# Layer A of an interleaved attention kernel: the third round's output scaled into the key tile, a value tail copy moved into the next segment, and the first Wo round moved behind the fourth Q

## The chip, the cores and the metric

The kernel runs on one core of a Trainium2 chip. Its metric is the device time of one execution in microseconds (us), and the median over several executions counts. One execution was also taken by the hardware profiler. Its page and its trace are what is read below. Engine names are those of the profile: PE (TensorE matmuls), PEld (its weight loads), DVE (VectorE), ACT (ScalarE), POOL (GpSimd), SP (SyncE, which here only issues DMAs).

## The reference

Four residual layers A, B, A, B work on x of 2048 rows by 640 columns. The change touches only layer A, a recurrent attention with 32 heads of 192 columns. Cut to what matters:

```python
for s in range(n_seg):                       # 64 segments of 32 rows, one after the other
    xs = x[:, s*32:(s+1)*32]                 # x is already layer-normed
    h = concatenate([mem, xs], axis=1)       # 8 memory rows + 32 rows
    q, k, v = h @ Wq, h @ Wk, h @ Wv         # per head
    p = softmax(where(mask, q @ k.T * scale, -1e9))
    o = (p @ v) @ Wo
    mem = o[:, :8]                           # the next segment needs this
    outs.append(o[:, 8:])
```

The memory rows make the 64 segments of a layer a serial chain: the first Q product of a segment cannot start before the Wo product of the segment ahead is complete.

## The kernel before

**Stages.** For each A layer `A_pre` projects, for all segments at once, the last 8 rows of each segment, which don't depend on the memory, and stores them in DRAM as `kqb` (Q and K) and `vb` (V). `A_chain` then runs the 64 segments. In a segment it handles 8 memory rows and the first 24 of the 32 rows, and takes the last 8 rows ("tails") from DRAM. The Wo product of the tails is made later in layer B from `otb`. Layer B is not touched.

**Rounds.** A segment has four rounds of eight heads, in the order 0, 1, 2, 3 in even and 3, 2, 1, 0 in odd segments. `order[0]` to `order[3]` name them here, and `L` is 3. Each round has a Q, a K and a V projection (`project`, L953, 20 matmuls each, with the stationary tile `hT`), scores (`scores`, L988 and L993), an exponential (`weigh`, L999), row sums (`sums`, L1004), the product with V (`attend`, L1018), reciprocals of the sums (`reciprocals`, a logarithm at L1009 and an exponential at L1010 on ACT), a scaling of the product into SBUF (`scale_out`, L1026 and twice L1030 on DVE) and a Wo product (`wo_round`, L1046, 24 matmuls) that accumulates over the four rounds in the PSUM tile `W`.

**Order.** The schedule is manual: each engine runs its instructions in the order of the program text, and waits are made from the data and from the reuse of tiles.

**Tiles.** Most tiles have a single buffer. `OT` (128 x 6 x 80) receives the scaled output of every round, feeds `wo_round`, feeds the tail copy of `store_tail` (L1035 on POOL, then a DMA), and holds the raw first Q of the next segment. `KT` (128 x 6 x 96) holds the transposed keys of the round. Its columns 0 to 63 are written by DVE (L968), and 16 of its columns 64 to 95 by POOL from `kqb` (`extra_kq`, L925, called by `next_kq`). `rc` holds the reciprocals, also in one buffer. `Vs` (named `Vp` in the profile) holds the values: partitions 0 to 63 those of the segment's own rows, 64 to 95 the tails in use, 96 to 127 the next tails from DRAM. `place_v` copies 96 to 127 down to 64 to 95 on POOL (L936) and issues the next fetch (`fetch_v`, L932). It runs twice in a segment.

**Weights.** Most of Wq, Wk and Wv stays in SBUF. Three of the five row blocks of each, for the first and the last round, share slots: as soon as the first round's projection has read a slot, SP loads the last round's piece into it (`load_slot`, L623). In the next segment the last round comes first. Wo works alike: rounds 1 and 2 are resident, rounds 0 and 3 share `wo_end`. After the first Wo round SP loads six pieces of the last round's rows (`load_wo`, L640, 320 KB each), which the fourth Wo round reads at the segment's end.

**Segment end.** After the last Wo round DVE transposes `W` (L1183), adds its halves into the first 8 columns of `hT` (L1186, four instructions with both inputs in SBUF), and the next segment's first Q can start. The first pair of L1186 releases its first 12 matmuls, the second pair the rest. `keep_busy` (L1054) puts matmuls whose result isn't used between the third and the fourth Wo round (8) and behind the fourth (16). The rows of a finished segment are added up at the start of the next by `keep_rows` (L905, L908) and stored by `store_rows` (L912, a DMA that POOL issues).

Of the kernel before, what the change touches and what calls it, by code (L numbers as in the profile page):

```python
# [115 lines left out]
class Kernel:  # L116
# [746 lines left out]
    def A_chain(self, xn_dram, at_dram, li, load_slot, piece, load_wo, late_wo, wo_mid, wo_end, low):  # L863
        nc, tc, KC, NSEG = self.nc, self.tc, self.KC, self.NSEG
        scale = float(self.Dh) ** -0.5
        NR = 4
        with tc.tile_pool(name=f"A{li}_ch", reuse_waits="tile", bufs=1) as sp, \
# [3 lines left out]
            KT = sp.tile([P, 6, 96], BF16, name="KT")  # L871
            QT = sp.tile([P, 2, 4, 80], BF16, name="QT")
            Vs = sp.tile([P, 896], BF16, name="Vp")
            OT = sp.tile([P, 6, 80], BF16, name="OT")
            for i, t in enumerate((KT, QT, Vs)):
                (nc.vector if i % 2 else nc.gpsimd).memset(t[:], 0.0)
            at_rows = self.attn_rows
# [33 lines left out]
            def store_rows(s, io):  # L911
                nc.gpsimd.dma_start(out=at_rows[32 * s:32 * s + 32, :].rearrange("t (g c) -> g t c", g=4), in_=io[:, :])  # L912
# [22 lines left out]
            def place_v():  # L935
                nc.gpsimd.tensor_copy(out=Vs[64:96, :], in_=Vs[96:P, :])  # L936
                fetch_v()
# [64 lines left out]
            def sums(S, E):  # L1002
                one = self.ones_blk[0:96, :]
                nc.tensor.matmul(S[:, 0:320], lhsT=ap3(one, [list(one.ap[0]), [0, P]]), rhs=E[0:96, 0:320], start=True,  # L1004
                                 stop=True, skip_group_check=True)
# [14 lines left out]
                                         stop=(k == 192), skip_group_check=True)  # L1020
                return O

            def scale_out(O, rc):
                rv = rc[:, :].rearrange("p (x e q) -> p x e q", e=2, q=80)
                ov = O[:, 0:480].rearrange("p (c q) -> p c q", q=80)
                nc.vector.tensor_tensor(out=OT[:, 0:4, :], in0=ov[:, 0:4, :],  # L1026
                                        in1=rc[:, :].rearrange("p (c q) -> p c q", q=80), op=ALU.mult)
                for e in range(2):
                    h = slice(64 * e, 64 * e + 64)
                    nc.vector.tensor_tensor(out=OT[h, 4:6, :], in0=ov[h, 4:6, :], in1=rv[h, :, e, :], op=ALU.mult)  # L1030

            def store_tail(s, r, tag="otb"):
                q0 = 64 - 64 * (r % 2)
                ob = sp.tile([P, 96], BF16, name="otb", tag=tag)
                nc.gpsimd.tensor_copy(out=ob[:, :].rearrange("p (c q) -> p c q", q=16), in_=OT[:, :, q0:q0 + 16])  # L1035
                nc.gpsimd.dma_start(out=self.otb_d[s, :, 96 * r:96 * r + 96], in_=ob[:, :])  # L1036

            def wo_round(W, r, first, last):
                m0 = 16 * (r % 2)
                w = wo_end[:, :] if r in (0, 3) else wo_mid[:, 7680 * (r - 1):7680 * r]  # L1040
                for j in range(0, 12, 2):
                    for g in range(4):
                        i = j + g // 2
                        G, c = (i // 4, i % 4) if i < 8 else (i % 4 // 2, 4 + i % 2)
                        wi = w[:, 640 * i:640 * i + 640].rearrange("p (h e c) -> p e h c", h=2, e=2)
                        nc.tensor.matmul(W[32 * g:32 * g + 32, 0:320], lhsT=OT[:, c, m0 + 32 * G:m0 + 32 * G + 32],  # L1046
                                         rhs=wi[:, g % 2], start=(first and j == 0), stop=(last and j == 10),
                                         tile_position=(0, 32 * g), skip_group_check=True)
# [33 lines left out]
            hx_transpose(hT, xr)  # L1082
            W = None
            for s in range(NSEG):
                order = rounds(s)
                L = NR - 1

                def q_or_k(m, n):
                    ps = pqp.tile([P, 512], F32, name="ps_qk", tag="qk")
                    project(hT, ps, m, n, s)  # L1090
                    return to_raw(ps, "raw" if n else "OT" if m == "Q" else "rc")

                def values(n, pool, tag):
                    pv = pool.tile([P, 512], F32, name="ps_v", tag=tag)
                    project(hT, pv, "V", n, s)
                    return pv

                if s > 0:
                    io = keep_rows(W)
                raw = q_or_k("Q", 0)  # L1100
                to_rows(raw, "Q", order[0])
                if s == 0:
                    fill(FILL[li])
                to_rows(q_or_k("K", 0), "K")
                if s == 0:
                    late_wo(2)
                if s > 0:
                    store_rows(s - 1, io)
                W = pop.tile([P, 512], F32, name="ps_w", tag="w")
                raw = q_or_k("Q", 1)  # L1110
                pv = values(0, pop, "v")
                v_rows(pv, 0, "s")
                v_rows(pv, 1, "s")
                S = scores(order[0])
                to_rows(raw, "Q", order[1])
                next_kq(s, 0)
                E = weigh(S)
                to_rows(q_or_k("K", 1), "K")
                for n in range(1, L):
                    raw = q_or_k("Q", n + 1)  # L1120
                    sums(S, E)
                    O = attend(E)
                    if n == 2:
                        place_v()
                    S1 = scores(order[n])
                    rc = reciprocals(S)
                    E = weigh(S1)
                    S = S1
                    to_rows(raw, "Q", order[n + 1])
                    next_kq(s, n)  # L1130
                    if n == 1 and s + 1 < NSEG:
                        xr = load_rows(s + 1)
                    if n == L - 1:
                        to_rows(q_or_k("K", n + 1), "K")
                        scale_out(O, rc)
                    else:
                        rawk = q_or_k("K", n + 1)
                        scale_out(O, rc)
                        to_rows(rawk, "K")
                    store_tail(s, order[n - 1])  # L1140
                    pv = values(n, pop, "v")
                    v_rows(pv, 0, "s")
                    v_rows(pv, 1, "s")
                    if n < L - 1:
                        wo_round(W, order[n - 1], n == 1, False)
                        if n == 1:
                            load_wo(order[L])
                            if s == NSEG - 1:
                                load_wo(3, low[:, 0:7680])
                pv = values(L, pqp, "qk")  # L1150
                sums(S, E)
                O = attend(E)
                S1 = scores(order[L])
                rc = reciprocals(S)
                E = weigh(S1)
                v_rows(pv, 1, "v")
                v_rows(pv, 0, "s")
                wo_round(W, order[L - 2], False, False)
                sums(S1, E)
                O1 = attend(E)  # L1160
                if s + 1 < NSEG:
                    hT = new_hT()
                    hx_transpose(hT, xr)
                scale_out(O, rc)
                store_tail(s, order[L - 1], "raw")
                next_kq(s, L)
                if s + 1 < NSEG:
                    place_v()
                wo_round(W, order[L - 1], False, False)
                rc = reciprocals(S1)  # L1170
                scale_out(O1, rc)
                idle = pop.tile([P, 512], F32, name="ps_idle", tag="v")
                keep_busy(idle, 2)
                wo_round(W, order[L], False, True)
                if s + 1 < NSEG:
                    keep_busy(idle, 4)
                store_tail(s, order[L])
                fill(SEG_FILL)
                if s + 1 < NSEG:
                    wt = sp.tile([P, 2, KC, 32], F32, name="wt", tag="rc")  # L1180
                    wv = W[:, 0:320].rearrange("p (h j b) -> p h b j", h=2, b=KC)
                    for b0, b1 in ((2, 5), (0, 2)):
                        nc.vector.transpose(out=wt[:, :, b0:b1, :], in_=wv[:, :, b0:b1, :])  # L1183
                        for h in range(2):
                            a, b = slice(64 * h, 64 * h + 64), slice(64 - 64 * h, 128 - 64 * h)
                            nc.vector.tensor_tensor(out=hT[a, b0:b1, 0:8], in0=wt[a, h, b0:b1, 0:8], in1=wt[b, h, b0:b1, 0:8],  # L1186
                                                    op=ALU.add)
# [72 lines left out]
```

## Time and profile before

| what | value |
|---|---|
| median of 3 runs | 3846.09 us (3836.32 to 3852.01) |
| profiled execution | 3840.06 us, span 3838.3 us |
| granted PE clock over the span | 0.98 |
| first chain: L1183, first and last start | 213.2 to 1588.1 us, 63 segments |
| second chain ends with its last Wo matmul at | 3534.8 us |
| PE busy in the span | 3457.9 us (90%) |
| DMA read and written | 853.72 MB and 73.40 MB, 242 GB/s over the span |

The two chains take some 2790 of 3838 us, and a segment takes about 22.2 us: (1588.1 - 213.2) us over 62 steps. What a change inside the segment brings is multiplied by 126, the number of steps from one segment to the next in both layers. The timeline of one engine lists its instructions in order of time. Its columns are start, duration, engine, line, operation, output and inputs, the shape, the number of merged instructions, and in brackets the idle time ahead of them with what ended it.

### The profile page before, as it was taken

What the parts mean: (1) busy time and instruction counts of PE and PEld (TensorE: products, weight loads), DVE (VectorE), ACT (ScalarE), POOL (GpSimd) and SP (SyncE); (2) the same over time, 40 slices, a digit from 0 to 9 for tenths busy, and PEclk for the clock granted to TensorE, in tenths of its full rate; (3) what the DMA queues carried; (4) which work ended last, traced back from release to release, by engine and by line L of the source; (5) the groups of instructions that cost most, each with busy time, mean ns of one, the idle gap of its engine ahead of it and who ended that gap; (6) DMA issues with size and microseconds to landing.
All of it is one profiled execution on the core that took longest, in us unless ns stands there. A gap on an engine that the chain in (4) does not pass through costs nothing. (4 is left out here: it accounts for less than half of the span.)

```text
span 3838.3 us, 147201 instructions
## 1 busy us (share of the span) xinstructions
PE 3457.9 (90%) x60042; PEld 2134.0 (56%) x60222; DVE 2243.8 (58%) x5940; ACT 1986.4 (52%) x4517; POOL 1958.4 (51%) x4871
## 2 busy tenths in 40 slices
PE   9989989989889989889899899998989899998898
PEld 6755555555555555555377555555555555555553
DVE  5456666666666666546633566666566666665465
ACT  2345555555555555545423455555555555555453
POOL 3455656655655656530433565565555565664300
PEclk9999999999999999999899999999999999999999
DMA  8978878788878878830477787887887788888300
GB/s 302 314 269 282 275 264 286 272 272 275 275 264 285 273 262 289 291 100 1 144 257 219 273 283 264 284 283 260 271 280 265 260 289 274 274 278 289 100 1 28
DMA packets 531681, 933.29 MB, mean 243 GB/s; under 512 B 145459, under 2 KB 295691, under 8 KB 531003
## 3 DMA queue, kind: packets, MB, share of 16 engines
q1 hardware_dynamic: 428858, 818.87, 61.9%
q0 software_dynamic: 68480, 91.75, 8.2%
q10 hardware_dynamic: 33664, 13.24, 1.4%
q8 instruction: 472, 7.73, 0.8%
q14 instruction: 207, 1.69, 0.1%
HBM read 853.72 MB, written 73.40 MB: 242 GB/s over the span
## 5 line engine op out<-in xcount | busy, mean ns | idle before, releaser
L953 PEld LDWEIGHTS <-hT 128*32 128x32 bf16 x30720 | 785.9, 96 | 654.2 <-DVE hT L1186 198.6
L953 PE MATMUL ps_qk<-arena,hT 128*32 128x384 bf16 x20480 | 992.3, 328 | 112.0 <-DVE hT L1186 96.5
L963 ACT ACTIVATE raw<-ps_qk 128x384 bf16<-128x384 f32 x896 | 440.0, 491 | 435.7 <-PE ps_qk L953 207.0
L1046 PE MATMUL ps_w<-arena,OT 128*32 128x320 bf16 x12288 | 549.9, 305 | 107.8 <-DVE OT L1026 68.8
L953 PE MATMUL ps_v<-arena,hT 128*32 128x384 bf16 x10240 | 503.3, 327 | 43.2 <-DMA arena<-in_A_Wv_dram 41.6
L980 ACT ACTIVATE Vp<-ps_v 64x384 bf16<-64x384 f32 x896 | 434.0, 484 | 72.2 <-PE ps_v L953 40.9
L972 DVE STREAM_TRANSPOSE QT<-raw 128x256 bf16<-128x256 bf16 x384 | 171.0, 445 | 489.9 <-PE ps_s L993 459.5
L1046 PEld LDWEIGHTS <-OT 128*32 128x32 bf16 x12288 | 260.2, 96 | 346.6 <-DVE OT L1026 168.7
L968 DVE STREAM_TRANSPOSE KT<-raw 128x384 bf16<-128x384 bf16 x512 | 296.2, 579 | 174.2 <-ACT raw L963 166.2
L916 POOL DMA_DIRECT2D kqb<-kqb x512 | 286.6, 560 | 163.9 <-POOL KT L925 115.4
L1036 POOL DMA_DIRECT2D otb<-otb x512 | 283.3, 553 | 169.6 <-POOL otb L1035 148.1
L1026 DVE TENSOR_TENSOR OT<-ps_o,rc 128x320 bf16<-128x320 f32 x512 | 251.8, 492 | 149.3 <-ACT rc L1010 55.2
L1030 DVE TENSOR_TENSOR OT<-ps_o,rc 64x160 bf16<-64x160 f32 x1024 | 324.7, 317 | 13.9
L905 ACT ACTIVATE half<-ps_w 64x160 f32<-64x160 f32 x256 | 76.4, 299 | 486.5 <-PE ps_qk L953 461.4
L922 POOL COPY QT<-kqb 128x64 bf16<-128x64 bf16 x512 | 121.9, 238 | 331.7 <-PE ps_s L993 326.0
L936 POOL COPY Vp<-Vp 32x896 bf16<-32x896 bf16 x256 | 237.4, 927 | 81.0 <-PE ps_o L1018 65.7
L1010 ACT ACTIVATE rc<-ps_s 128x320 f32<-128x320 f32 x512 | 224.0, 438 | 97.8 <-DVE OT L1030 86.8
L1009 ACT ACTIVATE ps_s<-ps_s 128x320 f32<-128x320 f32 x512 | 218.6, 427 | 102.6 <-PE ps_s L1004 99.1
L1035 POOL COPY otb<-OT 128x96 bf16<-128x96 bf16 x512 | 136.2, 266 | 260.1 <-DMA otb<-otb 104.4
L993 PE MATMUL ps_s<-QT,KT 128*96 128x80 bf16 (+1 forms) x3072 | 245.3, 218 | 19.9 <-DVE KT L968 2.4
L993 PEld LDWEIGHTS <-KT 128*96 128x96 bf16 x3072 | 222.1, 125 | 49.9 <-issue 41.5
L1018 PE MATMUL ps_o<-E,Vp 96*128 96x80 bf16 x4096 | 237.9, 203 | 0.5 <-POOL Vp L936 0.4
(156 smaller groups left out, 5444.5 us busy)
## 6 DMA issues: line engine op xcount, KB each, us to landing
arena<-wo_rows SPq DMA_DIRECT2D x792, 320.0 KB, 6.9
arena<-in_A_Wq_dram SPq DMA_DIRECT2D x427, 384.0 KB, 4.5
arena<-in_A_Wv_dram SPq DMA_DIRECT2D x427, 384.0 KB, 6.5
arena<-in_A_Wk_dram SPq DMA_DIRECT2D x768, 192.0 KB, 6.1
kqb<-kqb POOLq DMA_DIRECT2D x512, 48.0 KB, 5.0
arena<-in_A_Wk_dram SPq DMA_DIRECT2D x43, 384.0 KB, 6.7
vb<-arena POOLq DMA_DIRECT2D x128, 112.0 KB, 5.8
Vp<-vb POOLq DMA_DIRECT2D x256, 56.0 KB, 5.2
```

The source lines that it names most:

```text
L916: nc.gpsimd.dma_start(out=kqb[:], in_=self.kqb_d[s, :, r, :])
L936: nc.gpsimd.tensor_copy(out=Vs[64:96, :], in_=Vs[96:P, :])
L953: nc.tensor.matmul(ps[32 * g:32 * g + 32, 0:384], lhsT=hT[:, b, :], rhs=rhs, start=(i == 0), stop=(i == KC - 1), tile_position=(0, 32 * g) ...
L963: nc.scalar.activation(out=raw, in_=ps[:, 0:384], func=ACT.Copy)
L968: nc.vector.transpose(out=KT[:, :, 0:64], in_=raw.rearrange("p (c j) -> p c j", j=64))
L980: nc.scalar.activation(out=o, in_=i, func=ACT.Copy)
L993: nc.tensor.matmul(S[0:96, c0:c0 + 80 * (q1 - q0)], lhsT=KT[:, 3 * x + i, :], rhs=QT[:, x, q0:q1, :], start=False, stop=(x == 1 and i == 2 ...
L1018: nc.tensor.matmul(O[:, 80 * c:80 * c + 80], lhsT=Vs[0:96, 448 * x + k:448 * x + k + 128], rhs=E[0:96, 160 * x + 80 * e:160 * x + 80 * e + ...
L1026: nc.vector.tensor_tensor(out=OT[:, 0:4, :], in0=ov[:, 0:4, :], in1=rc[:, :].rearrange("p (c q) -> p c q", q=80), op=ALU.mult)
L1030: nc.vector.tensor_tensor(out=OT[h, 4:6, :], in0=ov[h, 4:6, :], in1=rv[h, :, e, :], op=ALU.mult)
L1036: nc.gpsimd.dma_start(out=self.otb_d[s, :, 96 * r:96 * r + 96], in_=ob[:, :])
L1046: nc.tensor.matmul(W[32 * g:32 * g + 32, 0:320], lhsT=OT[:, c, m0 + 32 * G:m0 + 32 * G + 32], rhs=wi[:, g % 2], start=(first and j == 0), ...
```

## The change

It has three parts, all in `A_chain`.

- `KO` names the columns 0 to 79 of `KT`. `scale_out`, `store_tail` and `wo_round` take the tile as an argument. The third round (`order[L - 1]`) uses `KO` in place of `OT`. Its scaling is placed ahead of the fourth round's `sums` and of the transposition into the new `hT`, and the reciprocals of the fourth round ahead of the third round's tail store and Wo. `next_kq(s, L)`, which writes columns of `KT`, goes behind the third Wo round in the text.
- The second `place_v` of a segment, with its fetch, moves from the segment's end to behind `store_rows` in the next segment.
- The first Wo round moves from behind the second round's V projection to behind the fourth Q projection (`q_or_k("Q", 3)`), one projection later on PE. The load of the last round's Wo pieces, which reuses its weights' buffer, moves with it.

No instruction is added or removed.

```diff
+            KO = KT[:, :, 0:80]
...
-            def scale_out(O, rc):
+            def scale_out(O, rc, OT=OT):
...
-            def store_tail(s, r, tag="otb"):
+            def store_tail(s, r, tag="otb", OT=OT):
...
-            def wo_round(W, r, first, last):
+            def wo_round(W, r, first, last, OT=OT):
...
                 if s > 0:
                     store_rows(s - 1, io)
+                    place_v()
...
                 for n in range(1, L):
                     raw = q_or_k("Q", n + 1)
+                    if n == 2:
+                        wo_round(W, order[0], True, False)
+                        load_wo(order[L])
+                        if s == NSEG - 1:
+                            load_wo(3, low[:, 0:7680])
                     sums(S, E)
                     O = attend(E)
...
                     v_rows(pv, 1, "s")
-                    if n < L - 1:
-                        wo_round(W, order[n - 1], n == 1, False)
-                        if n == 1:
-                            load_wo(order[L])
-                            if s == NSEG - 1:
-                                load_wo(3, low[:, 0:7680])
                 pv = values(L, pqp, "qk")
...
                 wo_round(W, order[L - 2], False, False)
+                scale_out(O, rc, KO)
                 sums(S1, E)
                 O1 = attend(E)
                 if s + 1 < NSEG:
                     hT = new_hT()
                     hx_transpose(hT, xr)
-                scale_out(O, rc)
-                store_tail(s, order[L - 1], "raw")
+                rc = reciprocals(S1)
+                store_tail(s, order[L - 1], "raw", KO)
+                wo_round(W, order[L - 1], False, False, KO)
+                scale_out(O1, rc)
                 next_kq(s, L)
-                if s + 1 < NSEG:
-                    place_v()
-                wo_round(W, order[L - 1], False, False)
-                rc = reciprocals(S1)
-                scale_out(O1, rc)
                 idle = pop.tile([P, 512], F32, name="ps_idle", tag="v")
                 keep_busy(idle, 2)
                 wo_round(W, order[L], False, True)
```

## The prediction, made before the changed kernel ran

> **What bounds the kernel now.** I read the page first.
>
> ```profile
> span 3838.3 us, 147201 instructions
> PE 3457.9 (90%) x60042; PEld 2134.0 (56%) x60222; DVE 2243.8 (58%) x5940; ACT 1986.4 (52%) x4517; POOL 1958.4 (51%) x4871
> DMA  8978878788878878830477787887887788888300
> ```
>
> PE leads, but DMA is busy too. So I next read single stretches of one segment, 701.95 to 723.65 us (first Q matmul to the next segment's). Columns: stretch, length, busy time of each engine, PE clock, DMA share, GB/s.
>
> ```profile
> 703.50:718.00 14.50, 13.80 (x293) 8.84 (x286) 8.03 (x22) 9.69 (x22) 8.62 (x24) 1.00 1.01 354
> 720.00:721.70 1.70, 1.39 (x36) 0.67 (x32) 1.05 (x4) 0.73 (x2) 0.72 (x2) 1.00 0.20 62
> 721.70:723.65 1.95, 1.69 (x40) 0.88 (x41) 1.28 (x6) 0.00 (x0) 1.49 (x7) 1.00 0.04 13
> ```
>
> DMA is saturated for most of the segment and idle at its end. The segment's Q matmuls start the stream of weights, and the sixth Wo piece ends it. So there are **two bounds in one loop**: PE with its hand-overs, and the weight stream. The waits of PE name both (total us, times, longest):
>
> ```profile
> PE ps_qk L953 <- DVE hT L1186: 96.5, 184, 1.0
> PE ps_w L1046 <- DVE OT L1026: 68.8, 154, 1.8
> PE ps_v L953 <- DMA arena<-in_A_Wv_dram: 41.6, 67, 3.1
> PE ps_w L1046 <- DMA arena<-wo_rows: 29.2, 58, 2.4
> ```
>
> One segment end on PE's timeline shows the order:
>
> ```profile
> 740.65 0.31 PE L1004 MATMUL ps_s<-E,few 96*128 96x320 bf16 x1
> 740.85 0.46 PE L1018 MATMUL ps_o<-E,Vp 96*128 96x80 bf16 x8
> 741.24 1.00 PE L1046 MATMUL ps_w<-arena,OT 128*32 128x320 bf16 x24
> 742.06 0.50 PE L1054 MATMUL ps_idle<-arena,ident 128*32 128x384 bf16 x8
> 742.83 0.90 PE L1046 MATMUL ps_w<-arena,OT 128*32 128x320 bf16 x20 [0.27 <-DVE OT L1026]
> 744.13 0.32 PE L1046 MATMUL ps_w<-arena,OT 128*32 128x320 bf16 x4 [0.40 <-DMA arena<-wo_rows]
> 745.97 0.35 PE L953 MATMUL ps_qk<-arena,hT 128*32 128x384 bf16 x4 [0.87 <-DVE hT L1186]
> ```
>
> The fourth Wo waits for `OT`, its last four matmuls for the sixth piece, the next Q for `hT`. The other engines there:
>
> ```profile
> 740.60 0.49 DVE L1026 TENSOR_TENSOR OT<-ps_o,rc 128x320 bf16<-128x320 f32 x1
> 741.76 0.44 ACT L1010 ACTIVATE rc<-ps_s 128x320 f32<-128x320 f32 x1 [0.35 <-DVE OT L1030]
> 742.29 0.49 DVE L1026 TENSOR_TENSOR OT<-ps_o,rc 128x320 bf16<-128x320 f32 x1 [0.62 <-PE ps_w L1046]
> 744.76 0.93 POOL L936 COPY Vp<-Vp 32x896 bf16<-32x896 bf16 x1
> 744.92 1.00 DVE L1186 TENSOR_TENSOR hT<-wt 64x24 bf16<-64x24 f32 x2
> ```
>
> The third scaling (740.60) follows the second Wo's read of `OT`; `rc` is rewritten only after it; the fourth scaling also waits for the third Wo. The pair of L1186 takes 1.00 us beside the value tail copy. Over the program:
>
> ```profile
> L1186 DVE TENSOR_TENSOR hT<-wt x504: 168/177/958, 213.6 to 3507.7; 64x24 bf16<-64x24 f32 x84, 64x16 bf16<-64x16 f32 x84
> ```
>
> **What the Trainium skill says.** "SBUF — State Buffer", Who interferes with whom: a DVE instruction with two SBUF inputs and a GpSimd one that reads SBUF exclude each other for a whole instruction. The trace agrees: L1186 stretches from 168 to 958 ns, while the transpose L1183 stays within 316 to 385. The same page puts HBM at about 358 GB/s for a core; the 354 GB/s above is there. "DMA: Bandwidth & Descriptors", Queues, rings and completion order: one issuer's descriptors are consumed in ring order. The page agrees: Wo and V pieces land 6.9 and 6.5 us after issue, a Q piece, first in the stream, 4.5.
>
> **The change part by part.**
>
> *Third output into KO.* From the fourth sums to the fourth Wo it is 2.18 us now (740.65 to 742.83), 2.51 in the mean over the trace's segments. With KO the third scaling waits for scores long done, not for the second Wo or POOL's tail copy, so `rc` is free in time and the third Wo's wait goes. What remains is the new chain: sums to logarithm 0.34 (740.65 to 740.99), logarithm to exponential 0.45, exponential 0.44, hand-over 0.1, L1026 and hand-over to PE 0.55: 1.88. PE's own work there, 0.2 + 0.39 + 0.82 + 0.33 of filler, is shorter. So the fourth Wo would start 1.88 after its sums, and the gain is 2.18 - 1.88 = 0.30 in the segment shown and 2.51 - 1.88 = 0.63 in the mean, which holds the segments where POOL's tail copy is late (it waits for the DMA of the copy ahead of it). The strided write into KT has the same element count as that into OT, and I take the same 0.49 for it; the trace of before has no such write, so between 0.4 and 0.6. On ACT and POOL nothing changes its place by this: the reciprocals and `next_kq` move in the text only, past work of other engines. The KT tail copy (L925) now waits for the third Wo, which ends before POOL gets to it: nothing. Scaling ahead of the `hT` transpose (0.37) is also covered; that transpose is needed only with the final L1186.
>
> *Value tail copy.* In the first chain between 220 and 1560 us the L1186 of 24 and 16 columns take 72.7 us for 240. At 0.177 each they would take 42.5: 30.2 us over 60 segments, 0.50 a segment. Behind `store_rows` the copy (0.93) and its fetch issue (0.51) lie on POOL in the gap before the next `extra_kq` (1.45 us idle at 706.84), beside bf16 transposes on DVE that never vary (L972 445 to 447 ns). If that gap closed, `extra_kq` would be late and hold the second scores, by up to 0.93 + 0.51 = 1.44 a segment. Queued behind it are the kqb fetch and the tail store, both with slack. The tail store now ahead of it frees `OT` earlier for the raw Q (0.1). But the store's own copy (0.26) may meet L1186: I take 0.05 lost, bounds 0 and 0.26. The fetch's 56 KB move into the saturated stretch: at 354 GB/s 0.16; I take 0.1.
>
> *First Wo later.* The step takes 0.94 in the mean where undisturbed it takes 0.84, so 0.1 of waiting goes, ahead of the V wait, which takes it back. On PE the round is moved past the fourth Q alone, whose raw copy to SBUF then has more time ahead of the scores. On SP the six Wo loads pass nothing (V of this segment is ahead, Q of the next behind), but are released about 0.85 later (one projection). V in front of them still has 3 to 5 us to land, so they queue anyway. Bound: 0 to 0.85. I take 0: in the quarter of segments that issue the first Wo piece latest (10.16 after the first Q, against 9.35 in the earliest) the first, third and fifth pieces land at 15.56, 17.52 and 19.44, against 15.65, 17.58 and 19.46.
>
> *Sum, and what is late next.* PE's side alone would gain 0.30 to 0.63 + 0.50 + 0.1 + 0.1, about 1.0 to 1.3 us. In the segment shown the KO part would bring the fourth Wo to 742.53, but its last four matmuls would still stand at 744.13, where their weights land: only the 0.6 us of the stretched L1186 would be won there. To get the mean, I followed the trace's landing times against each segment's first Q matmul. The sixth Wo piece lands 20.40 us after the first Q (mean of the 61 segments whose trace has it), and the next segment's Q never comes less than 1.25 after that (last four Wo matmuls, L1183, one pair of L1186). The mean is 1.78; a quarter of the segments are already at 1.25. So **the stream lets through only 1.78 - 1.25 = 0.53**, less 0.05 and 0.1: 0.38 a segment, times 126 is 48 us. Against the profiled 3840.06 this is 3792; the median shown lies 6 above it, so 3798.
>
> **Rivals.**
>
> *The Wo loads become late (slower).* If the sixth piece lands as much later as it is issued, 0.85, a segment gets -0.38 + 0.85 = 0.47 longer: 59 us, 3905. It decides against the change from 0.38 later landing on. For it: SP's queue stalls up to 1.77 us in one Wo issue. Against: the comparison of landings just shown.
>
> *The stream moves with PE (full gain).* If landings were paced by PE, all 1.0 to 1.3 would come: about 145 us, 3701. For it: K slots are released earlier. Against: 354 GB/s from 1.5 us on.
>
> *Nothing measurable.* The fetch and the tail copy cost their upper bounds (0.16, 0.26), or the scaling does not reach PE earlier: 0 to 0.1 a segment, 3840.
>
> **Numbers.** About 0.5%, 19 us, can be told from no change. Chances: forecast 0.72, full gain 0.05, nothing 0.11, slower 0.12. The forecast's own bounds are 0.53 plus up to 0.2 of earlier landing (92 us, 3754) and 0.1 (12 us, 3834); the range adds a little of the third rival. Faster 0.76 (forecast but 0.01, and full gain), same 0.12, slower 0.12.
>
> **What would show it.** Right: L1186 at most near 0.2 us, no wait of the fourth Wo for `OT` beyond some 0.3, and more Wo waits on `wo_rows` than 58. Wrong: a sixth landing later than 20.8; few DMA waits with a short segment (full gain); a new POOL wait ahead of the scores.

## The result, and the profile after

| kernel | median us (runs) | ratio to before, 95% interval |
|---|---|---|
| before | 3845.68 (4) | |
| changed | 3786.77 (4), 3775.47 to 3791.75 | 0.9845 (0.9814 to 0.9875) |
| changed, again beside 27 runs of before at 3837.95 | 3789.60 (5) | 0.9867 (0.9840 to 0.9894) |

The changed kernel is 48 to 59 us faster. The profiled execution took 3791.75 us with a span of 3790.0; before it was 3840.06 and 3838.3, 48 us more.

The page of the changed kernel (span, one engine line, the DMA slices, the chain by line):

```profile
span 3790.0 us, 147033 instructions
...
PE 3446.3 (91%) x60058; PEld 2175.8 (57%) x60222; DVE 2180.9 (58%) x5940; ACT 1999.4 (53%) x4517; POOL 1955.7 (52%) x4871
...
DMA  8988888888888888820477888888888888888300
...
DMA arena<-wo_rows 12%; PE ps_qk L954 9%; PE ps_v L954 3%; DMA arena<-in_A_Wv_dram 2%; PE ps_w L1047 2%; PE ps_qk L391 2%; PE ps_s L994 2%; PE ps_pre L825 1%; PEld L825 1%; DVE wt L1182 1%; PE ps_v L421 1%; DVE hT L1185 1%; PE kv L431 1%; PE ps_o L1019 1%; ACT arena L89 1%
```

PE's busy time hardly changes, in a span that is 48 us shorter. The Wo pieces head the chain that ended last (the chain on the page of before covers only a few per cent of the span, so the two can't be compared). The waits of PE (total us, times, longest) say more:

```profile
PE ps_w L1047 <- DMA arena<-wo_rows: 75.7, 157, 0.9
PE ps_v L954 <- DMA arena<-in_A_Wv_dram: 74.8, 108, 2.6
PE ps_qk L954 <- DVE hT L1185: 31.0, 128, 0.4
PE ps_s L994 <- POOL KT L926: 7.0, 7, 2.7
PE ps_w L1047 <- DVE OT L1027: 1.9, 5, 0.5
```

The wait for `OT`, 68.8 us before, is down to 1.9. That for `hT` fell from 96.5 to 31.0. The two waits on weights grew from 29.2 to 75.7 and from 41.6 to 74.8. The scores' wait for POOL grew too, from 2.1 to 7.0 us. A segment end on PE's timeline:

```profile
780.11 0.31 PE L1005 MATMUL ps_s<-E,few 96*128 96x320 bf16 x1
780.26 0.45 PE L1019 MATMUL ps_o<-E,Vp 96*128 96x80 bf16 x8
780.64 1.00 PE L1047 MATMUL ps_w<-arena,KT 128*32 128x320 bf16 x24
781.46 0.50 PE L1055 MATMUL ps_idle<-arena,ident 128*32 128x384 bf16 x8
781.98 1.14 PE L1047 MATMUL ps_w<-arena,OT 128*32 128x320 bf16 x20
783.61 0.32 PE L1047 MATMUL ps_w<-arena,OT 128*32 128x320 bf16 x4 [0.49 <-DMA arena<-wo_rows]
...
784.82 1.08 PE L954 MATMUL ps_qk<-arena,hT 128*32 128x384 bf16 x16 [0.24 <-DVE hT L1185]
```

The third Wo now reads `KT`. The fourth starts 1.87 us after its sums (780.11 to 781.98), where it took 2.18. Then its last four matmuls stand until 783.61 for the sixth piece, and 1.21 later the next segment begins. DVE's timeline at the same place:

```profile
779.49 0.49 DVE L1027 TENSOR_TENSOR KT<-ps_o,rc 128x320 bf16<-128x320 f32 x1
...
781.44 0.49 DVE L1027 TENSOR_TENSOR OT<-ps_o,rc 128x320 bf16<-128x320 f32 x1 [0.49 <-ACT rc L1011]
...
784.39 0.37 DVE L1185 TENSOR_TENSOR hT<-wt 64x24 bf16<-64x24 f32 x2
```

The third scaling no longer waits for the second Wo, and the fourth waits only for the reciprocals. The pair that took 1.00 us beside the tail copy takes 0.37. Over the program (minimum, median, maximum in ns):

```profile
L1185 DVE TENSOR_TENSOR hT<-wt x504: 168/176/303, 218.4 to 3463.8; 64x24 bf16<-64x24 f32 x84, 64x16 bf16<-64x16 f32 x84
```

### The profile page after: what moved, and what is told of

It reads as the page before. It is cut to its first block, busy times and chain, and to the rows that moved or that the text cites. A ratio compares the mean times of both kernels' runs of the same rounds, so it can differ in the third digit from the quotient of the medians.

```text
span 3790.0 us, 147033 instructions
## 1 busy us (share of the span) xinstructions
PE 3446.3 (91%) x60058; PEld 2175.8 (57%) x60222; DVE 2180.9 (58%) x5940; ACT 1999.4 (53%) x4517; POOL 1955.7 (52%) x4871
## 4 chain that ended last, share of the span: by engine, by line
PE 27%; DMA 16%; issue 5%; DVE 4%; ACT 3%; POOL 2%; PEld 2%; SPq 0%; POOLq 0%; DVEq 0%; ACTq 0%
DMA arena<-wo_rows 12%; PE ps_qk L954 9%; PE ps_v L954 3%; DMA arena<-in_A_Wv_dram 2%; PE ps_w L1047 2%; PE ps_qk L391 2%; PE ps_s L994 2%; PE ps_pre L825 1%; PEld L825 1%; DVE wt L1182 1%; PE ps_v L421 1%; DVE hT L1185 1%; PE kv L431 1%; PE ps_o L1019 1%; ACT arena L89 1%
## 5 line engine op out<-in xcount | busy, mean ns | idle before, releaser
L954 PE MATMUL ps_v<-arena,hT 128*32 128x384 bf16 x10240 | 515.6, 327 | 79.3 <-DMA arena<-in_A_Wv_dram 74.8
L1047 PE MATMUL ps_w<-arena,OT 128*32 128x320 bf16 x9216 | 428.1, 304 | 83.2 <-DMA arena<-wo_rows 75.7
L1047 PEld LDWEIGHTS <-OT 128*32 128x32 bf16 x9216 | 231.6, 97 | 249.6 <-issue 111.7
L1031 DVE TENSOR_TENSOR OT<-ps_o,rc 64x160 bf16<-64x160 f32 x768 | 243.0, 316 | 9.8
L1027 DVE TENSOR_TENSOR OT<-ps_o,rc 128x320 bf16<-128x320 f32 x384 | 188.6, 491 | 74.4 <-ACT rc L1011 58.6
L1019 PEld LDWEIGHTS <-Vp 96*128 96x128 bf16 x4096 | 210.0, 100 | 32.0 <-ACT Vp L981 13.6
L1000 ACT ACTIVATE E<-ps_s 96x320 bf16<-96x320 f32 x512 | 218.1, 426 | 12.3 <-PE ps_s L994 9.0
```

The lines of the kernel that those rows point to most:

```text
L954: nc.tensor.matmul(ps[32 * g:32 * g + 32, 0:384], lhsT=hT[:, b, :], rhs=rhs, start=(i == 0), stop=(i == KC - 1), tile_position=(0, 32 * g) ...
L1019: nc.tensor.matmul(O[:, 80 * c:80 * c + 80], lhsT=Vs[0:96, 448 * x + k:448 * x + k + 128], rhs=E[0:96, 160 * x + 80 * e:160 * x + 80 * e + ...
```

## The experiments

The theory was that the kernel before lost time in two hand-overs on PE's side (`OT`, and the tail copy against L1186), and that the weight stream lets only part of that come through. The table has, from each profiled execution's trace, when the Wo loads of a segment were issued and when the sixth piece landed (recorded in half of the segments), both from the segment's first Q, and the mean length of a segment (the first and last of each layer left out). All times are in us.

| kernel | first Wo piece issued (median) | sixth piece landed (mean) | segment (mean) |
|---|---|---|---|
| before | 9.58 | 20.40 | 22.16 |
| changed | 10.04 | 20.43 | 21.76 |
| tail copy alone | 9.35 | 20.33 | 21.84 |
| key tile alone | 9.36 | 20.29 | 21.90 |
| first Wo alone | 10.04 | 20.43 | 22.21 |
| tail copy and key tile | 9.35 | 20.48 | 21.74 |
| first Wo behind the scores | 11.2 | 21.00 | 22.30 |
| first Wo behind the fourth K | 12.5 | 22.09 | 23.48 |
| changed, fewer kqb loads | 10.04 | 19.95 | 21.21 |

**Tail copy alone.**

```diff
                     store_rows(s - 1, io)
+                    place_v()
...
                 next_kq(s, L)
-                if s + 1 < NSEG:
-                    place_v()
```

> The kernel before with one part of the change: the second value tail copy and its fetch go behind store_rows of the next segment. Theory (PE hand-overs under a cap set by the weight stream): L1186 falls from up to 958 ns to at most some 300, the sixth Wo piece still lands 20.4 us after the first Q, but the hand-over of OT stays, so the segment ends some 0.3 us earlier: 40 us less than before (25 to 55). Rival (full gain, the stream does not cap): 0.5 to 0.6 us a segment, 65 to 75 us less. Rival (the fetch in the saturated stretch costs what the copy gains): within 10 us of before.

Measured: 3799.53 us beside 3837.58, ratio 0.9898 (0.9879 to 0.9917), 38 us less. The hand-over of `OT` stays, as its waits show:

```profile
PE ps_w L1046 <- DVE OT L1026: 67.0, 163, 2.1
PE ps_w L1046 <- DMA arena<-wo_rows: 29.7, 61, 2.3
```

The tail copy's reader, by its own line (minimum, median, maximum in ns), is down to 174 ns and at most 310:

```profile
L1185 DVE TENSOR_TENSOR hT<-wt x504: 168/174/310, 218.6 to 3468.9; 64x24 bf16<-64x24 f32 x84, 64x16 bf16<-64x16 f32 x84
```

It is the size the theory gave (40), and neither the first rival's 65 to 75 nor the second's nothing.

**Key tile alone.**

```diff
+            KO = KT[:, :, 0:80]
...
+                scale_out(O, rc, KO)
                 sums(S1, E)
...
-                scale_out(O, rc)
-                store_tail(s, order[L - 1], "raw")
+                rc = reciprocals(S1)
+                store_tail(s, order[L - 1], "raw", KO)
+                wo_round(W, order[L - 1], False, False, KO)
+                scale_out(O1, rc)
                 next_kq(s, L)
                 if s + 1 < NSEG:
                     place_v()
-                wo_round(W, order[L - 1], False, False)
-                rc = reciprocals(S1)
-                scale_out(O1, rc)
```

> The kernel before with one part of the change: third round's output in the key tile, with its order of scaling, reciprocals, tail store and Wo. The value tail copy stays at the segment's end and the first Wo where it was. Theory: the fourth Wo starts about 1.9 us after its sums in place of 2.5, but the value tail copy on POOL keeps its time, so more of it falls on L1186, which takes part of the gain back: 25 us less than before (5 to 45), and more L1186 time than before's 150 us. The sum of this part and the copy's part is at least what both bring together. Rival (hand-overs add up): 0.30 to 0.63 us a segment, 38 to 79 us less.

Measured: 3816.98 us, ratio 0.9944 (0.9925 to 0.9962), 21 us less. The time came out as the theory had it, the rival's 38 to 79 fails, and 21 + 38 is at least what both parts bring together (53, below). But one reason of the theory did not hold. L1187, the same instruction, takes 128.6 us in all, less than the 150.1 of before and not more: the copy starts 1.21 us ahead of the next Q, where it was 1.01 (medians), which fits its meeting L1187 less. What holds the gain down is seen in the waits, where the one on weights has taken the place of that on `OT`:

```profile
PE ps_qk L954 <- DVE hT L1187: 72.2, 149, 1.0
PE ps_w L1047 <- DMA arena<-wo_rows: 71.2, 138, 2.8
```

**First Wo alone.**

```diff
                     raw = q_or_k("Q", n + 1)
+                    if n == 2:
+                        wo_round(W, order[0], True, False)
+                        load_wo(order[L])
...
-                    if n < L - 1:
-                        wo_round(W, order[n - 1], n == 1, False)
...
```

> The kernel before with one part of the change: the first Wo round and the six loads behind it go behind the fourth Q. Theory: the loads are issued 0.7 to 0.9 us later and land when they did, queued behind V: within 12 us of before. Rival (late Wo loads): the sixth piece lands up to 0.85 us later, and with half of the segments already waiting for it that costs 50 us or more.

Measured: 3850.08 us, ratio 1.0032 (1.0021 to 1.0042): 12.5 us slower, at the edge of the 12 that the theory allowed and far from the rival's 50.

```profile
PE ps_v L953 <- DMA arena<-in_A_Wv_dram: 64.1, 95, 2.6
PE ps_w L1046 <- DVE OT L1026: 59.9, 148, 1.7
```

The wait for `OT` fell by 9 us, and that for V grew by more, from 41.6 to 64.1. Why the part loses is open. Its profiled execution took 3843.51 us, less than its median, and only 3.5 more than the profiled one of before. In it the Wo loads that were issued late did not clearly land late: in the quarter of segments with the latest issue (10.82 on average) the fifth piece landed at 19.52, in the quarter with the earliest (10.03) at 19.51. The sixth landed at 20.58 against 20.33, but it is recorded in only 12 and 18 of the 30 segments, too few to tell.

**Tail copy and key tile, first Wo where it was.**

```diff
-                    if n == 2:
-                        wo_round(W, order[0], True, False)
-                        load_wo(order[L])
...
+                    if n < L - 1:
+                        wo_round(W, order[n - 1], n == 1, False)
+                        if n == 1:
+                            load_wo(order[L])
```

> The changed kernel with its third part undone: the first Wo and its loads are back behind the second V, key tile and tail copy stay changed. Theory: same as the changed kernel within 10 us, so 45 to 65 us less than before; the sixth piece lands at 20.4 and the next Q follows 1.25 later. Rival (the later first Wo matters, in one direction or the other): more than 15 us away from the changed kernel's 3787.

Measured: 3784.31 us, ratio 0.9859 (0.9837 to 0.9882). Again, on one chip with the changed kernel:

> The changed kernel itself, on the chip of the three others of this call: 45 to 65 us less than before. It stands here to be compared with the changed kernel without its third part.

> The changed kernel with the first Wo and its loads back behind the second V, again, now beside the changed kernel. Theory (the later release is still hidden, its saved wait is taken back by V): within 8 us of it. Rival (the later release already lets the queue run dry in some segments, as the part alone, 12 us slower, suggests): 8 to 15 us less than the changed kernel.

Measured: 3789.60 us (0.9867) for the changed kernel and 3783.71 us (0.9851, 0.9822 to 0.9880) without the third part. On this one chip the two are 6 us apart, within the theory's 8, with intervals that overlap widely. The first comparison is across chips and has the other sign by the ratios: 0.9845 for the changed kernel, 0.9859 without the third part. So the third part makes no difference, on top of the other two, that these runs can tell.

**Half of the Wo loads left out,** from the changed kernel and from before.

```diff
-                        load_wo(order[L])
+                        load_wo(order[L], part=range(3))
```

> The changed kernel without the loads of the last three of the six Wo pieces in each segment (the fourth Wo round multiplies with what stands there). It shortens the weight stream by 3 x 320 KB, 2.7 us at 354 GB/s, and nothing else. Theory (the stream caps the changed kernel, PE's own path is shorter by more than 1 us): the third piece lands near 17.7, no wait on wo_rows is left, and the segment falls from 21.7 to PE's path with its V waits, 20.4 to 20.7: 130 to 165 us less than the changed kernel, near 3640. Rival (the changed kernel is bound by PE and its hand-overs): within 30 us of the changed kernel's 3787.

> The kernel before without the loads of the last three of the six Wo pieces in each segment (the fourth Wo round multiplies with what stands there). Theory: before was bound by its hand-overs in most segments, so only its waits on wo_rows (29 us) go: 20 to 45 us less than before, near 3805. The distance to the same edit of the changed kernel is then what the hand-overs cost PE, 1.0 to 1.3 us a segment, 125 to 165 us. Rival (the stream bounds before as it does the changed kernel): both edits gain alike, 130 us or more.

Measured: 3681.34 us (ratio 0.9591, 0.9577 to 0.9606) from the changed kernel, and 3797.11 us (0.9892, 0.9875 to 0.9910) from before. The shorter stream brings the changed kernel some 100 us (97 to 106 by the ratios to before) and the kernel before 40. So the changed kernel is bound by the stream, and before was bound mostly by its hand-overs. The waits of PE, first of the edited before, then of the edited changed kernel:

```profile
PE ps_qk L953 <- DVE hT L1186: 98.2, 246, 1.0
PE ps_w L1046 <- DVE OT L1026: 79.0, 188, 1.9
PE ps_v L953 <- DMA arena<-in_A_Wv_dram: 16.3, 19, 2.5
```

```profile
PE ps_v L954 <- DMA arena<-in_A_Wv_dram: 61.9, 99, 2.4
PE ps_qk L954 <- DVE hT L1185: 37.4, 137, 0.4
```

With the end of the stream out of the way, the change is worth 3797.11 - 3681.34 = 116 us, 0.92 a segment. The two hand-over waits fell by more, 60.8 us on `hT` and 78.6 on `OT` (0.4 is left), together 1.11 a segment; the wait for V grew by 45.6 and took part of it back. The 100 us are less than the 130 expected, since PE's path with its V waits is 20.84 us long (mean of the trace) and not 20.4 to 20.7.

**The last Wo load left out.**

```diff
-                        load_wo(order[L])
+                        load_wo(order[L], part=range(5))
```

> The changed kernel without the load of the last of the six Wo pieces in each segment (the fourth Wo round multiplies with what stands there). Theory: the fifth piece, which lands at 19.6, now ends the stream; eight matmuls and the 1.2 us tail follow, so a segment takes some 21.0 in place of 21.75: 80 to 100 us less than the changed kernel, near 3697. Rival (bound by PE): within 20 us of the changed kernel.

Measured: 3696.96 us, ratio 0.963 (0.9614 to 0.9646), 83 to 91 us less than the changed kernel by the ratios to before. A piece less at the stream's end makes a segment 0.7 us shorter (21.08 on average), as the theory has it; the rival, bound by PE, fails.

**First Wo still later.** Behind the fourth K, and then half as far, behind the third round's scores.

```diff
                     raw = q_or_k("Q", n + 1)
-                    if n == 2:
-                        wo_round(W, order[0], True, False)
-                        load_wo(order[L])
...
                         to_rows(q_or_k("K", n + 1), "K")
+                        wo_round(W, order[0], True, False)
+                        load_wo(order[L])
```

> The changed kernel with the first Wo round and the loads behind it moved further, behind the fourth K: the loads are issued some 1.9 us later than in the changed kernel (near 12.0 after the first Q). Theory: V still fills the queue until about 15, so the sixth piece lands at 20.4 to 20.6 as before: within 20 us of the changed kernel's 3787. Rival (the release of the Wo loads sets their landing): up to 1.9 us a segment later, 100 us or more slower than the changed kernel.

Measured: 4009.25 us, ratio 1.0445 (1.0409 to 1.0480): 220 us slower than the changed kernel. The theory fell here. DMA's share in one segment (stretch, length, busy of the engines, PE clock, DMA share, GB/s; the segment begins at 801.68):

```profile
803.20:813.50 10.30, 10.17 (x216) 6.69 (x211) 5.91 (x17) 7.47 (x17) 6.74 (x17) 1.00 1.00 344
813.70:814.20 0.50, 0.50 (x24) 0.36 (x16) 0.47 (x3) 0.32 (x1) 0.50 (x1) 1.00 0.85 281
814.20:814.70 0.50, 0.50 (x21) 0.39 (x17) 0.04 (x1) 0.37 (x1) 0.21 (x2) 1.00 0.32 104
814.70:815.20 0.50, 0.50 (x24) 0.33 (x16) 0.34 (x1) 0.12 (x1) 0.46 (x2) 1.00 0.34 56
816.50:821.00 4.50, 4.23 (x89) 2.80 (x90) 3.04 (x9) 2.69 (x7) 2.82 (x9) 1.00 0.95 331
```

From about 12 us after the first Q the rate falls, to 104 GB/s at 12.5: most of the queued V is moved, though its last piece is reported landed at 14.5 (mean of the 63 segments that have it). The Wo loads, issued from 12.5, come too late to follow it, and PE waits for them:

```profile
PE ps_w L1047 <- DMA arena<-wo_rows: 238.9, 333, 3.1
```

The late loads are not the whole of the 220 us. The granted PE clock of the span is lower here as well, 0.980 in the changed kernel against

```profile
core 0: 4001.2 us, clock 0.948
```

In 90 of 120 segments the clock was halved for a stretch, 2.9 us long on average; in the changed kernel in one to three of 120. In the 30 segments at full clock the sixth piece landed at 21.22 and the segment took 22.63, 0.9 more than the changed kernel's 21.73 at full clock. Times 126 that is 113 us, an estimate. The rest came with the lower clock, and in those segments the Wo loads were also issued later (12.8 against 12.0). Whether the longer waits of PE brought the clock down is not shown.

The halfway place:

```diff
                     raw = q_or_k("Q", n + 1)
+                    sums(S, E)
+                    O = attend(E)
+                    if n == 2:
+                        place_v()
+                    S1 = scores(order[n])
                     if n == 2:
                         wo_round(W, order[0], True, False)
...
-                    sums(S, E)
-                    O = attend(E)
-                    if n == 2:
-                        place_v()
-                    S1 = scores(order[n])
                     rc = reciprocals(S)
```

> The changed kernel with the first Wo round and its loads behind the third round's scores: about 1.0 us later than in the changed kernel, half as far as behind the fourth K. Theory, revised after that run: weights already queued feed DMA only until about 12 us after the first Q, and a load needs some 1.3 us from issue to its data, so release is free up to an issue near 10.8 and then costs one for one; issued at 11.0 the sixth piece lands 0.1 to 0.4 later: 10 to 50 us slower than the changed kernel. Rival (one for one from where the changed kernel stands): 1.0 us a segment, 120 us slower. Rival (V's landing near 15 is the limit): no difference.

Measured: 3841.94 us, ratio 1.0015 (1.0003 to 1.0027), 52 us slower than the changed kernel beside it, just past the 10 to 50 of the theory. Both rivals fail (120 us, or nothing). The clock has a share here too, 0.971 over the span, with halved stretches in 34 of 120 segments. In the other 86, with the first Wo piece issued at 11.2 (median), the sixth landed at 20.72, 0.28 later than in the changed kernel at full clock (20.44), and the segment took 21.97, 0.24 longer: 30 us of the 52. Behind the fourth K, issued at 12.0 at full clock, it landed 0.78 later. A line through the two reaches no loss at about 10.8, an estimate. The changed kernel issues at 10.04.

**Fewer kqb loads.** Three of a segment's four kqb loads left out.

```diff
-                    extra_kq(kqs.pop(0), turns[at][1] % 2)
+                    kqb = kqs.pop(0)
+                    extra_kq(kqb, turns[at][1] % 2)
                     if at + 2 < len(turns):
-                        kqs.append(load_kqb(*turns[at + 2]))
+                        kqs.append(load_kqb(*turns[at + 2]) if n == L else kqb)
```

> The changed kernel without three of the four kqb loads of a segment (the tails' Q and K of those rounds are those of another round); the copies from the tile stay. 147 KB of small rows leave the stretch in which the stream runs. Theory (the stream caps): at 354 GB/s 0.4 us a segment, 50 us less than the changed kernel, 25 to 80 since these rows are short. Rival (such transfers fit beside the weights for nothing): within 10 us.

Measured: 3721.53 us, ratio 0.9686 (0.9658 to 0.9713), 68 us less than the changed kernel beside it. The rival (within 10 us) fails.

```profile
PE ps_w L1047 <- DMA arena<-wo_rows: 50.8, 127, 0.7
```

The sixth piece lands at 19.95, 0.5 earlier than in the changed kernel, and the segment follows. POOL issues three loads less as well, but the first Wo piece is issued at the same 10.04. So 147 KB of short rows cost 0.5 us of the stream, where 354 GB/s would make it 0.4.

## Why the prediction was right or wrong

The time was forecast at 3798 us and measured at 3787 and 3790, with the sign and the main mechanism, the stream as the cap, as forecast. One step, the first Wo, came near its value by luck. By its steps:

- **The cap.** It held to 0.03 us. The sixth piece landed at 20.43 where 20.40 was taken, and from there to the next Q it was 1.25 us from the 5th to beyond the 75th percentile of the segments. The segment became 0.40 us shorter; 0.38 was forecast. Leaving out Wo loads confirms the cap by taking it away.
- **The third output into KO.** The new distance from sums to the fourth Wo was put at 1.88 and is 1.87. The write into `KT` takes the same 0.49 us.
- **The value tail copy.** L1186 was to fall to its undisturbed time. It did, to 88.6 us in all, 0.176 each. The 0.05 a segment for the tail store's own copy was hardly lost: the maximum is 303 ns. A new POOL wait ahead of the scores, named as a sign of being wrong, did come, but with 5 us in the whole program: the gap on POOL nearly held.
- **PE's side alone.** 1.0 to 1.3 us a segment were forecast. Between the two half-Wo kernels the hand-over waits fell by 1.11, within that. The time fell by 0.92: the wait for V took 0.36 back, and smaller items, not traced, gave 0.17. The prediction had V take back only the 0.1 of the first Wo. It didn't matter, because the stream was the lower bound.
- **The first Wo later.** Here the working failed though its value, nothing, nearly held. The step read from V's landings that V "still has 3 to 5 us to land, so they queue anyway". The landing of a piece is not the end of its place in the queue: in the probe behind the fourth K the DMA rate fell from about 12 us on, with V reported landed at 14.5. The real margin is some 0.8 us (10.04 against about 10.8), and nothing in the prediction showed it. Its comparison of early and late segments reached only to 10.16, and it left out the sixth piece, which decides: in the trace of before that landed at 20.69 in the latest quarter against 20.20 in the earliest (14 and 12 segments have it), in the changed kernel's at 20.34 against 20.37. The rival of late Wo loads is a real mechanism that starts not far behind the changed kernel's place. Taken alone the part costs 12 us, and the cause of that is open.
- **The rivals.** Full gain falls with the half-Wo pair (116 us without the end of the stream, of which 48 to 59 came through). "Nothing measurable" falls with the ratio.

The expected median was 8 to 11 us too high. Profile and runs of the same kernel differ by as much (3775 to 3797 for the changed kernel), so no further term is looked for in it.

## What to carry to other kernels

When a loop feeds its own loads, look for two bounds and subtract them segment by segment: what a shorter engine path can bring is only the distance to the last load's landing plus what follows it. Before moving the release of a load, measure when the DMA share falls, not when the load ahead is reported landed. Read the granted clock before a slower run is put down to the edit alone. And once the stream is the bound, the small transfers beside it are the next place to look.

## What the runs showed of the hardware

- With three 48 KB loads of 384-byte rows per partition out of a saturated stretch, the last weight piece landed 0.5 us earlier, about 0.16 us for each load.
- A DVE addition with both inputs in SBUF took up to 0.96 us in place of 0.18 beside a 0.93 us POOL copy in SBUF. The transposes of the same stretch (L1183) stayed within a few ns of their time, and so did the bf16 transposes from SBUF to SBUF (L972, 445 to 447 ns, 121 of 384 beside such a copy).
- The last V load of a segment was reported landed some 2 us after the DMA rate had fallen from about 350 GB/s to 104 (first Wo behind the fourth K: the fall is read in the segment shown, at 12.5 us after the first Q, and the landing, 14.5, is the mean).
- In the mean over the changed kernel's segments each half us from 2.5 to 17.5 us after the first Q had 304 to 389 GB/s, so the 354 of one stretch is a mean and not a ceiling.
- Two kernels in which PE waited longer for Wo (239 and 129 us in all, against 76) had a lower granted PE clock, 0.948 and 0.971 against 0.980. That one brings the other is not shown.
